# x turned by a transposing DMA, the last keys' values paired otherwise, and the adapter's output product at another place

## The chip, the cores and the metric

The kernel runs on one core of a Trainium2 chip. The metric is the device time of one execution in microseconds (us); every time below is in us unless ns stands beside it. The engines are PE (matmul; PEld is its weight load), DVE (vector), ACT (scalar, exponentials), POOL (general) and SP, which in this kernel only issues DMAs.

## The reference

Attention with a relative position bias, for 8 batches, 8 heads, 576 positions and head width 64; then a mixture of low-rank adapters on the 4608 rows of 512 that it gives.

```python
scores = q @ k.T / sqrt(64) + bias_table[bucket(|i - j|)]
attn = softmax(scores)                          # over the keys
x = (attn @ v) laid out as (8 * 576, 512)
logits = x @ w_gate                             # 8 experts
w = softmax of the two largest logits           # the two experts kept
out = x + sum over the two of w * ((x @ A[e]) @ B[e])   # A: 512 x 16, B: 16 x 512
```

## The kernel before

The work is cut into 32 **units**, u = 4 b + hp, of one batch b and one pair of heads hp. Of the 576 positions of a batch 512 are the main part, in four tiles of 128, and 64 are the tail. The scores are computed with the keys on the partitions: `keys(u, c)` gives a block of 128 keys against 512 queries of both heads (tile `sc`, L353 and L358; the bias enters as a product with a table), `keys_exp` its exponential on ACT (`pk`, L364). `edges(u)` gives the scores of tail keys and tail queries (L395, L400) and their exponential `pt` (L402), which `edge_bias` corrects on POOL (L408) and DVE (L410).

Score tiles take turns in three PSUM buffers of two banks, six tiles a unit: two `keys`, a third, the turning of the next unit's q and k (`tp`), the fourth `keys`, and the next unit's `edges`. All else that PE writes goes to the pool `mp` (tag `mm`) of two buffers with one bank each: values (`pv`), the adapter's output product (`dl`), the corner scores (`cps`), turned x (`xT_ps`), logits of a whole group (`zl`).

The values, attn @ v with a column of ones for the sums, are computed a unit late, in two groups. `values_a` (tiles 0, 1, 2) and `values_b` (tile 3 and the tail) each fill one `pv` tile; `pv_main` (L418) adds a block of main keys, `pv_last` (L428) the tail keys, `pv_tail` (L442) is for the tail's queries. Tiles 0 and 2 can share a weight load in `pv_last`, as can 1 and 3, since tail keys of two batches lie on the two halves of the partitions. `normalise_a` and `normalise_b` divide by the sums on DVE and write x: `xs[b]` for the main part, `xe[b // 2]` for the tails of two batches.

The adapter works on **groups**: two tiles of x (g0: tiles 0 and 1; g1: 2 and 3), or the tail rows of two batches. For each group x is turned (`turn_x`, L334, and `copy_x`, L338), multiplied with the first adapter matrices and the gate (`moe_z`, L499, in the free columns of a `pv` tile from `values_b`, or `moe_zpair`, L507), gated on DVE, POOL and ACT, and turned again (`moe_t`, L559, `moe_tc`, L562); `moe_d` (L566, L569) makes the output product `dl`, adds x and, when a group is complete, issues the store on SP's queue.

The order of everything is written out by hand in the loop over u; the engines take their instructions in that order. Dictionaries hold which group's step comes in which unit. With u the first unit of batch b, `moe(b - 1, u)` puts the steps of batch b - 1 there: g0 is turned in unit u + 1, g1 in u + 2, a tail group in u + 3; `moe_z` for the four tiles comes in u + 2 to u + 5, `moe_d` (dictionary `second`) in u + 5 to u + 8. For batch 6 the turns come in u and u + 1, each followed by `moe_zpair` at the end of the same unit. Batch 7 is done after the loop, in code that the change does not touch.

In a unit, the order on PE is: two `keys`; `moe_d`; `values_b` of the unit before with `moe_z`; transposes of x; the third `keys`; the turning of q and k (and `cps` in a batch's first unit); the fourth `keys`; `values_a` of the unit before with `moe_t`; `edges` of the next unit. In unit 28 `values_a` comes directly behind `values_b`.

SP issues in program order the loads of q and k four units ahead and of v three units ahead, the tails a batch ahead, and the stores. A DMA whose data is not ready holds up all behind it.

## Time and profile before

| | |
|---|---|
| median of three runs | 205.93 us (204.39 to 206.39) |
| profiled execution, its own time | 205.11 us |
| span of its profile | 203.3 us |
| granted PE clock | 0.998 of full speed |
| PE, PEld busy | 173.8, 127.5 us (86%, 63%) |
| ACT, DVE, POOL busy | 166.1, 138.3, 130.9 us (82%, 68%, 64%) |
| moved by DMA | 39.87 MB, mean 196 GB/s |

The span runs from the first to the last instruction of the profiled execution; the 1.8 us between it and the execution's own time lie around it. A busy share is a mean over stages. Idle time of an engine stands in the profile with the releaser, the instruction that ended it; the chain is followed back from the last instruction through these releasers.

### The profile page before, as it was taken

What the parts mean: (1) busy time and instruction counts of PE and PEld (TensorE: products, weight loads), DVE (VectorE), ACT (ScalarE), POOL (GpSimd) and SP (SyncE); (2) the same over time, 40 slices, a digit from 0 to 9 for tenths busy, and PEclk for the clock granted to TensorE, in tenths of its full rate; (3) what the DMA queues carried; (4) which work ended last, traced back from release to release, by engine and by line L of the source; (5) the groups of instructions that cost most, each with busy time, mean ns of one, the idle gap of its engine ahead of it and who ended that gap; (6) DMA issues with size and microseconds to landing.
All of it is one profiled execution on the core that took longest, in us unless ns stands there. A gap on an engine that the chain in (4) does not pass through costs nothing.

```text
span 203.3 us, 11419 instructions
## 1 busy us (share of the span) xinstructions
PE 173.8 (86%) x4898; PEld 127.5 (63%) x4898; DVE 138.3 (68%) x411; ACT 166.1 (82%) x205; POOL 130.9 (64%) x321
## 2 busy tenths in 40 slices
PE   0377889899999899989988999999988997999870
PEld 0255666677666677766676677767776685666640
DVE  4314655467667876887877777789877786888750
ACT  3269999998998889989879889889988878788470
POOL 4298546678578647986694947985776577761110
PEclk9999999999999999999999999999999999999999
DMA  5868889679778886855279999862498940042165
GB/s 134 214 192 240 235 243 240 177 212 272 213 208 254 252 218 203 242 173 158 58 196 299 280 242 295 251 203 72 108 280 262 291 167 24 3 157 107 55 241 173
DMA packets 62714, 39.87 MB, mean 196 GB/s; under 512 B 17848, under 2 KB 59336, under 8 KB 62664
## 3 DMA queue, kind: packets, MB, share of 16 engines
q1 hardware_dynamic: 61864, 38.58, 64.7%
q8 instruction: 38, 0.62, 1.3%
q10 hardware_dynamic: 800, 0.56, 1.1%
q14 instruction: 12, 0.10, 0.2%
HBM read 29.67 MB, written 9.46 MB: 192 GB/s over the span
## 4 chain that ended last, share of the span: by engine, by line
PE 51%; ACT 18%; DVE 15%; issue 5%; DMA 5%; POOL 2%; ACTq 0%; POOLq 0%; DVEq 0%
PE pv L418 14%; PE sc L353 10%; ACT pk L364 10%; ACT pt L402 6%; PE sc L358 5%; DVE ot L569 5%; PE xT_ps L334 4%; PE pv L428 3%; PE sc L395 3%; PE tp L302 3%; DVE pt L410 2%; PE sc L400 2%; PE dl L566 2%; PE pv L442 2%; DMA Wt<-g_d 1%
## 5 line engine op out<-in xcount | busy, mean ns | idle before, releaser
L364 ACT ACTIVATE pk<-sc 128x1024 bf16<-128x1024 f32 x128 | 124.1, 1028 | 14.6 <-PE sc L358 13.4
L353 PE MATMUL sc<-qkT 64*64 64x512 bf16 x512 | 52.8, 396 | 3.4 <-ACT pk L364 2.7
L418 PEld LDWEIGHTS <-pk 128*128 128x128 bf16 x1024 | 38.7, 98 | 16.4 <-issue 7.8
L358 PE MATMUL sc<-Wt,anti 64*64 64x384 bf16 (+1 forms) x512 | 44.1, 300 | 1.8 <-DMA Wt<-g_d 1.8
L418 PE MATMUL pv<-v,pk 128*128 128x65 bf16 x992 | 42.7, 194 | 0.9 <-DVE z L522 0.4
L402 ACT ACTIVATE pt<-sc 128x1024 bf16<-128x1024 f32 x32 | 32.8, 1024 | 10.3 <-PE sc L400 5.2
L306 DVE COPY qkT<-tp 128x1024 bf16<-128x1024 bf16 x32 | 22.0, 686 | 6.9 <-PE tp L302 6.2
L410 DVE TENSOR_TENSOR pt<-pt,ET 64x256 bf16<-64x256 bf16 x32 | 15.3, 477 | 15.2 <-ACT pt L402 11.9
L353 PEld LDWEIGHTS <-qkT 64*64 64x64 bf16 x512 | 17.1, 106 | 12.7 <-issue 5.7
L137 POOL CAST v<-vs 128x512 bf16<-128x512 f32 x32 | 20.4, 637 | 6.6 <-DMA vs<-in_v_dram 6.5
L141 POOL CAST kn<-ks 128x512 bf16<-128x512 f32 x31 | 19.4, 626 | 1.1 <-PE sc L358 0.9
L358 PEld LDWEIGHTS <-anti 64*64 64x64 bf16 x512 | 17.9, 108 | 2.9 <-issue 2.9
L569 DVE TENSOR_TENSOR ot<-dl,xn 128x512 f32<-128x512 f32 x25 | 17.3, 691 | 1.3 <-PE dl L566 0.3
L477 DVE TENSOR_TENSOR xn<-pv,rc 128x384 bf16<-128x384 f32 x31 | 17.3, 557 | 1.1
L141 POOL CAST qn<-qs 128x512 bf16<-128x512 f32 x27 | 16.6, 613 | 1.6 <-PE sc L358 0.9
L428 PE MATMUL pv<-vb,pt 128*128 128x65 bf16 (+1 forms) x186 | 17.5, 203 | 0.0
L302 PEld LDWEIGHTS <-qn 64*64 64x64 bf16 x512 | 10.8, 111 | 10.4 <-ACT qn L141 5.3
L532 POOL TENSOR_TENSOR a<-z,top 128x16 f32<-128x16 f32 (+1 forms) x17 | 3.8, 223 | 19.2 <-DVE top L527 19.1
L302 PE MATMUL tp<-ident,qn 64*64 64x64 bf16 x512 | 11.1, 196 | 5.7 <-ACT qn L141 5.3
L562 DVE COPY zT<-pv 128x128 bf16<-128x128 bf16 x31 | 6.7, 221 | 12.0 <-PE pv L559 12.0
L408 POOL TENSOR_TENSOR pt<-pt,ELC 128x128 bf16<-128x128 bf16 x32 | 13.8, 431 | 1.5 <-ACT pt L402 1.4
L442 PE MATMUL pv<-v,pt 128*128 128x65 bf16 x248 | 13.0, 193 | 0.0
(147 smaller groups left out, 337.8 us busy)
## 6 DMA issues: line engine op xcount, KB each, us to landing
qs<-in_q_dram SPq DMA_DIRECT2D x32, 256.0 KB, 3.9
vs<-in_v_dram SPq DMA_DIRECT2D x64, 128.0 KB, 4.0
ks<-in_k_dram SPq DMA_DIRECT2D x62, 128.0 KB, 3.8
out_dram<-ot SPq DMA_DIRECT2D x11, 512.0 KB, 4.2
vt<-in_v_dram SPq DMA_DIRECT2D x8, 128.0 KB, 4.1
out_dram<-fot SPq DMA_DIRECT2D x4, 256.0 KB, 2.4
qkt<-in_q_dram SPq DMA_DIRECT2D x7, 128.0 KB, 4.7
qkt<-in_k_dram SPq DMA_DIRECT2D x7, 128.0 KB, 3.9
```

Of the source, the lines that this page charges most:

```text
L137: eng.tensor_copy(t[:, :, :, :D].rearrange("p c h d -> p h c d"), s)
L141: copy(t.rearrange("p c h d -> p h c d"), s)
L302: nc.tensor.transpose(self.ps[h * 64:h * 64 + 64, f, x * 64:x * 64 + 64], src[rows, h * 64:h * 64 + 64], ident[rows, rows])
L306: nc.vector.tensor_copy(_ap(dst, 0, [[64, 2], [128, n], [1, 64]]), self.ps[:, :, x * 64:(x + n) * 64].rearrange("p f (x t) -> p f x t", t=64))
L353: nc.tensor.matmul(sc[prt, h, :], lhsT=kT[rows, c * 128 + f * 64:c * 128 + f * 64 + 64], rhs=qT[rows, :], start=True, stop=False, skip_gro ...
L358: nc.tensor.matmul(_ap(sc[prt, h, :], p0, [[128, 4], [1, n]]), lhsT=turned(h), rhs=_ap(Wt[rows, hp, :], (1 - e) * GY + y0, [[GY, 4], [1, n]]),
L364: nc.scalar.activation(probs[u][0][c], scs.pop(c), ACT.Exp, scale=scale)
L402: nc.scalar.activation(probs[u][1][:, 64:], sc.rearrange("p h x -> p (h x)"), ACT.Exp, scale=scale)
L410: eng.tensor_tensor(te, te, ET[64:, :, hp, :], op=ALU.mult)
L418: nc.tensor.matmul(pv[:, o + h * W1:o + (h + 1) * W1], lhsT=pk[c][:, h, t * 128:(t + 1) * 128], rhs=vm[:, c, h, :], start=(first and h == ...
L428: nc.tensor.matmul(_ap(pv, o + h * W1, [[260, n], [1, W1]]), lhsT=pt[:, x0:x0 + 128], rhs=tvs[b % 2][:, t // 2:t // 2 + n, 2 * hp + h, :], ...
L569: nc.vector.tensor_tensor(gr.ot[:, t, :], dl, gr.x[t], op=ALU.add)
```

## The change

Three edits come together.

1. `turn_x` issues one transposing DMA on SP's queue, from x in SBUF to `xT` in SBUF. The transposes on PE, their PSUM tile `xT_ps` and `copy_x` on DVE go. The place in the program order stays.
2. `values_a` does tiles 0 and 2 and the tail's queries, `values_b` tiles 1 and 3, so that each has one `pv_last` with shared weight loads. The normalising is divided in the same way.
3. The dictionary `second`, that is `moe_d`, runs after the fourth `keys`, ahead of `values_a`, instead of ahead of `values_b`.

```diff
     def turn_x(gr):
         n = len(gr.x)
-        gr.xT_ps = mp.tile([128, 2, 4, 128], BF16, name="xT_ps", tag="mm")
-        for i, x in enumerate(gr.x):
-            for c in range(4):
-                nc.tensor.transpose(gr.xT_ps[:, i, c, :], x[:, c * 128:(c + 1) * 128], ident)
-
-    def copy_x(gr):
-        gr.xT = xtp.tile([128, len(gr.x), 4, 128], BF16, name="xT", tag="xT")
-        nc.vector.tensor_copy(gr.xT, gr.xT_ps[:, :len(gr.x)])
+        gr.xT = xtp.tile([128, n, 4, 128], BF16, name="xT", tag="xT")
+        nc.sync.dma_start_transpose(out=gr.xT.rearrange("p n c t -> p (n c) t"), in_=gr.flat)
...
     def pv_last(u, pv, o, t, n=1):
...
-            nc.tensor.matmul(_ap(pv, o + h * W1, [[260, n], [1, W1]]), lhsT=pt[:, x0:x0 + 128],
+            nc.tensor.matmul(_ap(pv, o + h * W1, [[130, n], [1, W1]]), lhsT=pt[:, x0:x0 + 128],
...
     def values_a(u):
         pva[u] = mp.tile([128, 512], FP32, name="pv", tag="mm")
-        for t in range(3):
+        for t in (0, 2):
             for c in range(4):
-                pv_main(u, pva[u], t * 130, t, c, t == 0 and c == 0)
+                pv_main(u, pva[u], t * W1, t, c, t == 0 and c == 0)
         pv_last(u, pva[u], 0, 0, 2)
-        pv_last(u, pva[u], 130, 1)
+        for c in range(5):
+            pv_tail(u, pva[u], c, 260)
         return pva[u]
 
     def values_b(u):
         pvb[u] = mp.tile([128, 512], FP32, name="pv", tag="mm")
-        for c in range(4):
-            pv_main(u, pvb[u], 0, 3, c, c == 0)
-        pv_last(u, pvb[u], 0, 3)
-        for c in range(5):
-            pv_tail(u, pvb[u], c)
+        for t in (1, 3):
+            for c in range(4):
+                pv_main(u, pvb[u], (t - 1) * W1, t, c, t == 1 and c == 0)
+        pv_last(u, pvb[u], 0, 1, 2)
         return pvb[u]
...
+    def norm_pair(u, pv, rc, t, i):
+        b, hp = units[u]
+        nc.vector.tensor_tensor(_ap(xs[b], t * Dm + hp * 128, [[2 * Dm, 2], [D, 2], [1, D]]),
+                                _ap(pv, 0, [[2 * W1, 2], [W1, 2], [1, D]]),
+                                _ap(rc, i, [[2, 2], [1, 2], [0, D]]), op=ALU.mult)
+
     def normalise_a(u):
...
-        nc.vector.tensor_tensor(_ap(xs[b], hp * 128, [[Dm, 3], [D, 2], [1, D]]),
-                                _ap(pv, 0, [[2 * W1, 3], [W1, 2], [1, D]]),
-                                _ap(rc, 0, [[2, 3], [1, 2], [0, D]]), op=ALU.mult)
+        norm_pair(u, pv, rc, 0, 0)
+        rows = slice(64 * (b % 2), 64 * (b % 2) + 64)
+        nc.vector.tensor_tensor(xe[b // 2][rows, hp * 128:hp * 128 + 128].rearrange("p (h d) -> p h d", h=2),
+                                _ap(pv[rows], 260, [[W1, 2], [1, D]]), _ap(rc[rows], 4, [[1, 2], [0, D]]),
+                                op=ALU.mult)
 
     def normalise_b(u):
...
-        nc.vector.tensor_tensor(_ap(xs[b], 3 * Dm + hp * 128, [[D, 2], [1, D]]),
...
+        norm_pair(u, pv, rc, 1, 6)
...
             gr.x = [xs[b][:, c, :] for c in (2 * i, 2 * i + 1)]
+            gr.flat = xs[b][:, 2 * i:2 * i + 2, :].rearrange("p c d -> p (c d)")
...
             gr.x = [xe[b // 2]]
+            gr.flat = xe[b // 2]
...
         if u == 6:
             weights_turn(1)
-        run(second.pop(u - 1, []))
...
             if early:
                 normalise_a(u - 1)
-            else:
-                for gr in xg:
-                    copy_x(gr)
...
             run(after.pop(u, []))
+            run(second.pop(u - 1, []))
             if not early:
                 pa = values_a(u - 1)
             else:
                 for gr in xg:
                     turn_x(gr)
-                    copy_x(gr)
```

More of the change, by code (lines that the diff above doesn't have):

```diff
@@ L427, in pv_last, with pv_tail @@
             x0 = 64 + h * SM + 256 + t % 2 * 128
-            nc.tensor.matmul(_ap(pv, o + h * W1, [[260, n], [1, W1]]), lhsT=pt[:, x0:x0 + 128],
+            nc.tensor.matmul(_ap(pv, o + h * W1, [[130, n], [1, W1]]), lhsT=pt[:, x0:x0 + 128],
                              rhs=tvs[b % 2][:, t // 2:t // 2 + n, 2 * hp + h, :], start=False, stop=False,
                              skip_group_check=True)
-    def pv_tail(u, pv, c, o=130, first=False):
+    def pv_tail(u, pv, c, o, first=False):
         b, hp = units[u]
@@ L484, in normalise_b @@
         nc.vector.reciprocal(rc[:, 6:], _ap(pv, D, [[W1, 4]]))
-        nc.vector.tensor_tensor(_ap(xs[b], 3 * Dm + hp * 128, [[D, 2], [1, D]]),
-                                _ap(pv, 0, [[W1, 2], [1, D]]),
-                                _ap(rc, 6, [[1, 2], [0, D]]), op=ALU.mult)
-        rows = slice(64 * (b % 2), 64 * (b % 2) + 64)
-        nc.vector.tensor_tensor(xe[b // 2][rows, hp * 128:hp * 128 + 128].rearrange("p (h d) -> p h d", h=2),
-                                _ap(pv[rows], 130, [[W1, 2], [1, D]]), _ap(rc[rows], 8, [[1, 2], [0, D]]),
-                                op=ALU.mult)
+        norm_pair(u, pv, rc, 1, 6)
     class Group:
```

## The prediction

> **What bounds the kernel now.** I read the page first (busy shares, the chain by line), then the stretches between two units, then the chain in order of time, last SP's queue.

> ```profile
> span 203.3 us, 11419 instructions
> PE 51%; ACT 18%; DVE 15%; issue 5%; DMA 5%; POOL 2%; ACTq 0%; POOLq 0%; DVEq 0%
> ```

> No engine bounds it alone: the chain changes between PE, ACT and DVE. So the unit of account is one unit of the loop (one batch and head pair). Each ends with the 24 matmuls of `values_a` (L418), which stand in the chain and serve as a clock; unit 17's start at 107.14, unit 20's at 123.53. Stretches between such marks (columns: PE, PEld, DVE, ACT, POOL busy, clock, DMA share, GB/s):

> ```profile
> 52.72:57.72 5.00, 4.66 (x148) 3.39 (x146) 3.48 (x12) 4.69 (x7) 2.87 (x9) 1.00 0.68 179
> 107.14:112.99 5.85, 5.26 (x150) 3.82 (x148) 4.39 (x13) 5.08 (x7) 3.50 (x10) 1.00 1.00 300
> 112.99:118.49 5.50, 5.05 (x161) 3.79 (x160) 3.91 (x13) 4.95 (x6) 3.82 (x8) 1.00 0.93 286
> 118.49:123.53 5.04, 5.03 (x149) 3.55 (x148) 4.05 (x13) 4.71 (x7) 2.84 (x9) 1.00 0.86 219
> 123.53:129.15 5.62, 5.62 (x154) 4.31 (x152) 4.14 (x14) 5.08 (x8) 5.23 (x14) 1.00 0.97 297
> ```

> A unit that turns x (5.85, 5.50, 5.62) is 0.5 to 0.8 longer than one that does not (5.00, 5.04). The chain says why. First a short unit, then a turning one:

> ```profile
> 52.20 0.41 PE sc L353 x4
> 52.61 0.11 PE sc L358 x2
> 52.72 0.93 PE pv L418 x24
> 53.65 0.18 PE pv L428 x4
> 53.83 0.23 PE sc L395 x4
> 54.06 0.12 PE sc L400 x16
> ...
> 55.21 1.95 ACT pk L364 x2
> ...
> 57.20 0.41 PE sc L353 x4
> ```
> ```profile
> 109.83 0.68 DVE pt L410
> ...
> 110.54 0.70 DVE ot L569
> ...
> 111.28 0.61 PE xT_ps L334 x8
> 111.89 0.34 PE sc L353 x4
> ```

> In the short unit two legs follow each other. On PE: the last `keys` (0.52), `values_a` (1.11), `edges` (0.35). On ACT: the exponential of the edges and the first two of the keys, after which a score tile is free for the last `keys` again. ACT itself stands idle ahead of the edges, so the PE leg counts in full:

> ```profile
> 54.29 1.02 ACT L402 ACTIVATE pt<-sc 128x1024 bf16<-128x1024 f32 x1 [0.31 <-POOL sm L536]
> ```

> The releaser named there is POOL; I read it as the edges' matmuls, which end at 54.18. In the turning unit another way is longer: edges' exponential, DVE's product on it, then `ot` behind it, which frees the misc PSUM tile that the transposes need.

> ```profile
> PE xT_ps L334 <- DVE ot L569: 5.7, 11, 0.7
> L338 DVE COPY xT<-xT_ps 128x1024 bf16<-128x1024 bf16 (+1 forms) x17 | 10.7, 630 | 1.0 <-PE xT_ps L334 1.0
> ```

> **The change, part by part.**

> *Transposes and copies removed.* Each full group takes 0.61 off PE and one copy off DVE (17 copies, 10.7 us). DVE's time is worth nothing by itself. What it is worth on the path is the difference between a turning unit and what bounds the unit next. Were that 5.04, units 9 to 27 (57.72 to 162.14, 104.4 us for 19) would lose 8.6.

> *The product `dl` moved.* Now it stands between the first two `keys` and `values_b`, where PE waits for DVE's product on the edges anyway: unit 20 has it there and takes 5.04. After the change it stands between the last `keys` and `values_a`, on the PE leg of the loop, in every unit from 9 to 31. Its cost there is its step in the chain, and the short transpose of `zt` adds 0.06:

> ```profile
> 121.00 0.32 PE dl L566
> 119.58 0.06 PE pv L559
> ```

> So a unit becomes 5.00 + 0.34 + 0.06 = 5.40, whether it turns x or not. In the first unit of a batch a second price comes: the misc pool has two buffers, and there `pv`, `cps` and now `dl` come ahead of `values_a`. One of the last two must take the buffer of `cps`, which is free only when ACT has read it:

> ```profile
> 122.94 1.03 ACT L364 ACTIVATE pk<-sc 128x1024 bf16<-128x1024 f32 x1
> 123.51 0.95 PE L418 MATMUL pv<-v,pk 128*128 128x65 bf16 x24
> 123.84 0.41 ACT L376 ACTIVATE pcx<-cps 128x256 bf16<-128x256 f32 x1
> ```

> ACT leaves it at 124.25. PE would be through `dl` at 123.51 + 0.34 = 123.85, so it waits 0.4 to 0.5; such a unit (12, 16, 20, 24) becomes 5.86. Sum over units 9 to 27: 15 x 5.40 + 4 x 5.86 = 104.4, what they take now. The saving of the turning units is spent on the others. Below, `dl` could be worth nothing (5.04 stays); above, 0.39, its whole duration. I take the chain's step.

> *Values paired.* `values_a` has 24 + 4 = 28 matmuls now and 16 + 2 + 10 = 28 after; `values_b` goes from 20 to 18, ahead of a wait. DVE's pieces are regrouped (three ops and four, as now). Zero, bounds -0.05 and +0.05 a unit.

> *The DMA.* No transposing DMA is in this trace. Nearest rows, from issue to landing:

> ```profile
> qs<-in_q_dram SPq DMA_DIRECT2D x32, 256.0 KB, 3.9
> vt<-in_v_dram SPq DMA_DIRECT2D x8, 128.0 KB, 4.1
> out_dram<-fot SPq DMA_DIRECT2D x4, 256.0 KB, 2.4
> ```

> The load of q has the size of a turn of two tiles; `vt` moves runs of 256 bytes, as a turn does (128 values of 2 bytes). The lower bound is 2.4, a quiet queue; the upper 8.2, two transfers like `vt` one after the other. I take 3.9 on a busy queue and 2.4 on an idle one. In most batches this is hidden: x is ready just after a batch's first unit, its consumer `moe_z` comes over a unit later. It is not hidden where SP comes late, since the DMA is issued behind the loads of its unit:

> ```profile
> 98.88 1.19 SPq L578 DMA_DIRECT2D out_dram<-ot  x2
> ...
> 105.70 0.42 SPq L589 DMA_DIRECT2D out_dram<-ot  x1
> 106.21 0.39 SPq L113 DMA_DIRECT2D qs<-in_q_dram  x1
> ...
> 108.32 1.06 SPq L110 DMA_DIRECT2D vs<-in_v_dram  x2
> 110.29 0.40 PE L499 MATMUL pv<-AW,xT 128*128 128x136 bf16 x4
> ```

> SP waits for the tail's `ot` until 98.88, then works through unit 16's eight loads and a store until 106.1 and unit 17's loads until 109.4; only there would the turn of batch 3 be issued. That is 11.6 after the edges' exponential of unit 16 (97.77). Two units of 5.86 and 5.40, and 1.85 to `moe_z` in unit 18, give 13.1. Room 1.5, need 3.9: PE stands 2.4 if SP is as slow as now, about 1.2 if longer units take the back-pressure off SP (its loads took 3.2 where 2.5 is their sum undisturbed). I take 1.8, and 2.2 for batch 5, where SP's same stretch is 0.5 longer. Everything behind `moe_z` on PE (two `keys`, the turning of q and k) waits too, then ACT, so it counts in full. Batch 5's tail is turned and used in the same unit 27: 0.8, the rest lies beside ACT.

> Batch 6 is turned in unit 28 and used at its end:

> ```profile
> 165.89 0.36 SPq L589 DMA_DIRECT2D out_dram<-ot  x1
> 168.99 0.61 PE L334 MATMUL xT_ps<-ident,xn 128*128 128x128 bf16 x8 [0.70 <-ACT pcx L376]
> 169.63 0.69 DVE L338 COPY xT<-xT_ps 128x1024 bf16<-128x1024 bf16 x1 [0.97 <-PE xT_ps L334]
> 170.38 0.65 PE L507 MATMUL zl<-AW,xT 128*128 128x136 bf16 x8 [0.37 <-DVE xT L338]
> ```

> The store at 165.89 belongs to a product that moves behind the last `keys`, to some 169.4, and the turn is queued behind it: issue at 169.8, landing at 172.2 against 170.38, +1.8. Unit 29 drops 0.6 of transposes from a PE that is busy throughout, unit 6 the 0.5 that it has in the chain:

> ```profile
> 46.19 0.45 PE xT_ps L334 x8
> ```

> Sum: 0 - 0.5 - 0.6 + 1.8 + 2.2 + 0.8 + 1.8 = +5.5. The profiled execution took 205.11 (span 203.3 and 1.8 around it), 0.8 below the median 205.93. 205.1 + 5.5 = 210.6; I say 210.5, and leave the 0.8 to the range.

> The row of q gives 3.9 for a plain 256 KB. [...]

> **Rivals.** *In time, and the product hidden* (faster): landing near 2.4, and `dl` finds idle time on PE, as it does in unit 20 now. Then units take 5.04, minus 8.6, minus 0.5 (unit 6), minus 0.6 (unit 29), plus 1.8 in unit 28: 197. For it: PE is 4.66 busy in 5.00. Against: ACT's idle time ahead of the edges shows that PE's leg has no slack. It holds if units fall below 5.2.

> *In time, product on the path*: units at 5.40, landing 2.4, so the late places cost 0.3, 0.7, 0 and 1.8, less 1.1: 206.8. For it: the queue can be that quick after the loads thin out. Against: DMA share 1.00 at 107 to 113, just there.

> *Slow turns*: landing 6 to 8.2. Units 18, 26 and 28 wait 2 to 6 longer each; units 14 and 22, where the turn is issued some 3 after the unit before begins and 7.3 ahead of `moe_z`, wait 1.7 to 3.9; in units 6 and 10, issued at 0.9, at most 1.8: 221 to 236. For it: 17 more transfers of many short runs. Against: `vt` lands in 4.1 with runs as short.

> *No effect at all*: the turn is not done by DMA, or PE still carries the transposes: 2%.

> **How the numbers follow.** Forecast 40%, faster rival 22%, product on the path but in time 18%, slow turns 18%, no effect 2%. About 1% is what a measurement of this kernel can tell from no change (203.9 to 208.0). Faster: 0.22. Same: 0.20. Slower: 0.58. The likeliest case alone has 207 to 214 (landing 3 to 5); the range that reaches to the others is 197 to 220 and leaves out the slow turns.

> **What would show it.** Right: the short chain in every unit with `dl` between `sc` L353 and `pv` L418; units of 5.3 to 5.5, batches' first units near 5.9 with a wait for `pcx`; PE at `moe_z` in units 18 and 26, and at `zl` in unit 28, waiting for the DMA that writes `xT`; landing 3 to 5. Wrong: units near 5.05, no wait for `xT`, or such waits in every batch.

## The result, and the profile after

| | before | after |
|---|---|---|
| median | 206.16 us (204.39 to 206.82, 4 runs) | 235.53 us (232.03 to 236.23, 4 runs) |
| ratio, 95% interval | 1 | 1.133 (1.124 to 1.142) |
| profiled execution, its span | 205.11, 203.3 us | 235.47, 233.6 us |
| granted PE clock | 0.998 | 0.937 |

The changed kernel takes 29 us more by the medians of all runs, and 27 by the ratio, which leaves out the executions that fell into a slower state. 210.5 had been forecast, with 197 to 220 as the range. The page of the changed kernel gives the first hint: the busy times of PE and ACT have hardly moved (173.8 to 178.0 and 166.1 to 165.9), but the transfer that writes `xT` stands in the chain that ended last, and the clock has dips.

```profile
span 233.6 us, 11065 instructions
PEclk9999999988999999799995999999985995899998
PE 41%; DMA 19%; ACT 18%; DVE 7%; issue 6%; POOL 3%; SPq 2%; ACTq 0%; POOLq 0%
```

DMA had 5% of the chain before and has 19% now. The waits by PE's lines (total, times, longest) say where it stands, and the list of DMA issues how long the transfer is (KB are not given for it; the last number is the median time from issue to landing):

```profile
PE pv L497 <- DMA xT<-xn: 18.3, 5, 5.6
PE zl L505 <- DMA xT<-xn: 4.6, 1, 4.6
PE zl L505 <- DMA xT<-xe: 1.0, 1, 1.0
```
```profile
xT<-xn SPq DMA_TRANSPOSE x14, 4.6
xT<-xe SPq DMA_TRANSPOSE x3, 3.6
```

Seven of the 17 turns are late for their reader (`moe_z`, L497, and `moe_zpair`, L505), by 23.9 in all. The five at L497 stand in units 6, 14, 18, 22 and 26. Below, the length of a unit u is the time from the start of the exponential of its edges to that of the next unit's, read from ACT's timeline of each kernel.

| unit | before | after | e1 | e2 | e4 | e5 | e8 |
|---|---|---|---|---|---|---|---|
| 6 | 5.86 | 11.03 | 5.85 | 12.02 | 6.20 | 8.56 | 7.92 |
| 14 | 5.78 | 8.58 | 5.72 | 7.46 | 5.52 | 5.21 | 6.36 |
| 18 | 5.80 | 12.43 | 5.58 | 12.03 | 5.22 | 10.30 | 5.22 |
| 22 | 5.58 | 6.20 | 5.72 | 8.36 | 5.21 | 5.22 | 7.02 |
| 26 | 5.80 | 12.08 | 5.22 | 11.46 | 5.79 | 10.36 | 5.22 |
| 28 | 6.32 | 6.84 | 7.18 | 8.09 | 5.79 | 5.79 | 13.54 |
| 29 | 6.44 | 12.03 | 6.73 | 7.14 | 6.18 | 11.96 | 12.70 |
| 9 to 27 | 104.4 | 120.9 | 104.2 | 115.5 | 105.1 | 113.2 | 106.3 |

(e1: x turned on PE again; e2: the transposing DMA alone; e4: nothing waits for `xT`; e5: turn issued ahead of the loads; e8: stores later as well. All are told below.) After against before, the span grows by 30.3: unit 6 +5.2, 14 +2.8, 18 +6.6, 22 +0.6, 26 +6.3, units 28 to 30 +6.7, the other 15 units from 9 to 27 +0.2 together, what follows unit 30 +1.9.

Unit 18 shows what such a wait does. First PE, with the idle time and its releaser in brackets; then stretches of two microseconds (behind the length of the stretch stand the busy times of PE, PEld, DVE, ACT and POOL; the last three numbers are granted clock, DMA share, GB/s):

```profile
117.67 0.28 PE L423 MATMUL pv<-vb,pt 128*128 128x130 bf16 x2
123.52 0.64 PE L497 MATMUL pv<-AW,xT 128*128 128x136 bf16 x4 [5.58 <-DMA xT<-xn]
126.05 0.61 PE L564 MATMUL dl<-Bc,zT 128*128 128x512 bf16 x1
```
```profile
118.00:120.00 2.00, 0.00 (x0) 0.00 (x0) 0.00 (x0) 1.57 (x3) 0.22 (x1) 1.00 0.90 252
122.00:124.00 2.00, 0.48 (x4) 0.36 (x4) 0.00 (x0) 0.00 (x0) 0.54 (x1) 0.52 1.09 275
124.00:126.00 2.00, 2.00 (x50) 1.08 (x48) 1.29 (x4) 0.85 (x1) 0.61 (x2) 0.50 1.11 250
128.00:130.00 2.00, 2.00 (x54) 1.41 (x52) 0.94 (x4) 0.96 (x2) 0.62 (x1) 0.77 0.88 272
```

PE stands 5.58, and then works at half the clock until some time after 128: `dl` takes 0.61 where it takes 0.39 elsewhere. Unit 18 is 12.43, where a unit of its kind without a wait is 5.26 (unit 17); 7.2 lost for a wait of 5.6. On SP's queue the turn of that batch (its issue at 118.40) stands behind this:

```profile
101.55 0.93 SPq L110 DMA_DIRECT2D vs<-in_v_dram  x2
106.98 2.04 SPq L576 DMA_DIRECT2D out_dram<-ot  x2
...
114.94 0.35 SPq L588 DMA_DIRECT2D out_dram<-ot  x1
...
117.36 0.93 SPq L110 DMA_DIRECT2D vs<-in_v_dram  x2
118.40 2.37 SPq L333 DMA_TRANSPOSE xT<-xn  x1
```

SP issues nothing between 102.5 and 107.0 (it stands at the store of a tail, L576), has three tail loads, ten unit loads and another store to issue, and reaches the turn at 118.40, when PE has already been standing for its result since 117.94.

A unit that waits for no x looks as forecast. The chain in unit 10, the waits for `cps`, and the stretches of units 10 and 12 (the second is a batch's first unit; in it, at 84.58, PE waits 0.40 for ACT to have read `cps`):

```profile
70.77 1.94 ACT pk L359 x2
...
72.75 0.41 PE sc L348 x4
73.16 0.11 PE sc L353 x2
73.27 0.37 PE dl L564
73.64 0.51 PE pv L413 x16
```
```profile
PE pv L413 <- ACT pcx L371: 1.6, 4, 0.4
```
```profile
69.85:75.06 5.21, 4.74 (x144) 3.32 (x139) 3.44 (x12) 4.78 (x6) 3.13 (x8) 1.00 0.94 146
80.38:86.16 5.78, 5.04 (x146) 3.51 (x139) 3.45 (x12) 5.06 (x7) 3.60 (x9) 1.00 0.75 167
```

### The profile page after: what moved, and what is told of

The parts are those of the page before. It is cut to its first block, busy times and chain, and to the rows that moved or that the text cites. A ratio compares the mean times of both kernels' runs of the same rounds, so it can differ in the third digit from the quotient of the medians.

```text
span 233.6 us, 11065 instructions
## 1 busy us (share of the span) xinstructions
PE 178.0 (76%) x4711; PEld 125.3 (54%) x4712; DVE 126.4 (54%) x394; ACT 165.9 (71%) x205; POOL 131.2 (56%) x321
## 4 chain that ended last, share of the span: by engine, by line
PE 41%; DMA 19%; ACT 18%; DVE 7%; issue 6%; POOL 3%; SPq 2%; ACTq 0%; POOLq 0%
ACT pk L359 14%; DMA xT<-xn 11%; PE sc L348 10%; PE pv L413 10%; PE sc L353 5%; PE pv L437 4%; PE dl L564 3%; PE sc L390 2%; SPq L110 2%; DMA vs<-in_v_dram 2%; PE pv L423 2%; DMA xT<-xe 2%; PE pv L497 2%; DVE qkT L306 1%; PE tp L302 1%
## 5 line engine op out<-in xcount | busy, mean ns | idle before, releaser
L348 PE MATMUL sc<-qkT 64*64 64x512 bf16 x512 | 55.4, 415 | 8.2 <-ACT pk L359 7.6
L353 PE MATMUL sc<-Wt,anti 64*64 64x256 bf16 (+1 forms) x512 | 46.3, 315 | 2.2 <-DMA Wt<-g_d 2.2
L413 PE MATMUL pv<-v,pk 128*128 128x65 bf16 x992 | 44.1, 197 | 3.2 <-ACT pcx L371 1.6
L348 PEld LDWEIGHTS <-qkT 64*64 64x64 bf16 x512 | 18.9, 110 | 19.1 <-issue 12.2
L471 DVE TENSOR_TENSOR xn<-pv,rc 128x256 bf16<-128x256 f32 x62 | 26.3, 424 | 2.1
L497 PE MATMUL pv<-AW,xT 128*128 128x136 bf16 x96 | 10.4, 235 | 18.3 <-DMA xT<-xn 18.3
L488 DVE RECIPROCAL rc<-pv 128x4 f32<-128x4 f32 x31 | 5.7, 184 | 30.5 <-PE pv L497 22.2
L353 PEld LDWEIGHTS <-anti 64*64 64x64 bf16 x512 | 18.9, 112 | 3.0 <-issue 2.9
L405 DVE TENSOR_TENSOR pt<-pt,ET 64x256 bf16<-64x256 bf16 x32 | 12.0, 374 | 13.3 <-ACT pt L397 9.7
L423 PE MATMUL pv<-vb,pt 128*128 128x130 bf16 x124 | 17.8, 226 | 0.0
L497 PEld LDWEIGHTS <-xT 128*128 128x128 bf16 x96 | 6.8, 102 | 19.2 <-DMA xT<-xn 19.2
## 6 DMA issues: line engine op xcount, KB each, us to landing
qs<-in_q_dram SPq DMA_DIRECT2D x32, 256.0 KB, 4.1
vs<-in_v_dram SPq DMA_DIRECT2D x64, 128.0 KB, 4.1
ks<-in_k_dram SPq DMA_DIRECT2D x62, 128.0 KB, 3.8
vt<-in_v_dram SPq DMA_DIRECT2D x8, 128.0 KB, 3.9
out_dram<-fot SPq DMA_DIRECT2D x4, 256.0 KB, 4.7
qkt<-in_q_dram SPq DMA_DIRECT2D x7, 128.0 KB, 3.3
qkt<-in_k_dram SPq DMA_DIRECT2D x7, 128.0 KB, 3.8
```

The lines of the kernel that those rows point to most:

```text
L348: nc.tensor.matmul(sc[prt, h, :], lhsT=kT[rows, c * 128 + f * 64:c * 128 + f * 64 + 64], rhs=qT[rows, :], start=True, stop=False, skip_gro ...
L353: nc.tensor.matmul(_ap(sc[prt, h, :], p0, [[128, 4], [1, n]]), lhsT=turned(h), rhs=_ap(Wt[rows, hp, :], (1 - e) * GY + y0, [[GY, 4], [1, n]]),
L413: nc.tensor.matmul(pv[:, o + h * W1:o + (h + 1) * W1], lhsT=pk[c][:, h, t * 128:(t + 1) * 128], rhs=vm[:, c, h, :], start=(first and h == ...
L423: nc.tensor.matmul(_ap(pv, o + h * W1, [[130, n], [1, W1]]), lhsT=pt[:, x0:x0 + 128], rhs=tvs[b % 2][:, t // 2:t // 2 + n, 2 * hp + h, :], ...
L471: nc.vector.tensor_tensor(_ap(xs[b], t * Dm + hp * 128, [[2 * Dm, 2], [D, 2], [1, D]]), _ap(pv, 0, [[2 * W1, 2], [W1, 2], [1, D]]), _ap(rc ...
L497: nc.tensor.matmul(zl, lhsT=gr.xT[:, t, c, :], rhs=AW[:, c, :], start=False, stop=(c == 3), skip_group_check=True)
```

## The experiments

**The three edits apart.** e1 takes the first edit back and leaves the other two; e2 has the first alone; e3 the second alone.

e1_pe_turn, against the changed kernel:

```diff
     def turn_x(gr):
-        nc.sync.dma_start_transpose(out=gr.xT..., in_=gr.flat)
+        (transposes on PE into xT_ps, copy_x on DVE, as before)
```

> The changed kernel with x turned on PE and copied by DVE again; pairing and the product's new place stay. Theory (the turn by DMA comes late and PE waits for it): no wait of 4 to 6 is left, time 205 to 212, PE's clock 1.0 throughout; a turning unit takes 5.5 to 6.0, the others 5.2 to 5.3, first units of a batch 5.8. Rival (the product's place or the pairing costs the 30): 225 or more.

Measured: 209.74 us (209.19 to 210.31), ratio 1.016 (1.010 to 1.023). Units 9 to 27 take 104.2 against 104.4 before; units 28 to 30 are 1.7 longer, and unit 0 is 1.2 longer in this profile.

e2_dma_only, against the kernel before: only `turn_x` by DMA, `copy_x` gone.

> The kernel before with the turn by DMA alone; pairing and the product's place as before. Theory: the waits for xT in units 6, 14, 18, 22, 26 and 28 stay, 225 to 235; units without a wait take 5.0 to 5.1, since no product stands on PE's leg. Rival (product's place or pairing costs the 30): 200 to 208.

Measured: 225.20 us (221.76 to 227.71). Of the units from 9 to 27 those without a late turn take 5.00 to 5.06 (but 5.31 in unit 16 and 5.39 in unit 24), and seven readers wait, five of them at `moe_z`:

```profile
PE pv L493 <- DMA xT<-xn: 20.3, 5, 6.0
```

e3_pair_only, against the kernel before: `values_a` with tiles 0 and 2 and the tail, `values_b` with 1 and 3.

> The kernel before with the pairing of the values alone. As forecast: two matmuls fewer in values_b, ahead of a wait, and the same number in values_a: 205 to 207, no difference that can be told. Rival (pairing shortens or lengthens every unit by 0.1 or more): 203 or 209.

Measured: 206.93 us (205.83 to 210.12), ratio 1.007 (1.003 to 1.010). In its profile units 9 to 27 are the same to 0.02; the 1.3 that its unit 0 takes more stands in the start-up, as in e1.

What follows: the loss is the DMA's; the two others cost one or two per cent together. In e2 the 15 units from 9 to 27 that are not 14, 18, 22 or 26 save 5.3, where the bound of 5.04 a unit gives 5.9; so the transposes were worth about what had been worked out, and the waits cost several times as much.

**The transfer, or the wait for it.** e4 lets every turn be issued as in the changed kernel, but nobody reads its result.

```diff
-            nc.tensor.matmul(zl, lhsT=gr.xT[:, t, c, :], rhs=AW[:, c, :], start=False,
+            nc.tensor.matmul(zl, lhsT=sel[:, c * 128:(c + 1) * 128], rhs=AW[:, c, :], start=False,
...
-                nc.tensor.matmul(zl[:, t, :], lhsT=gr.xT[:, t, c, :], rhs=AW[:, c, :],
+                nc.tensor.matmul(zl[:, t, :], lhsT=sel[:, c * 128:(c + 1) * 128], rhs=AW[:, c, :],
```

> The changed kernel, but the products that make the logits read a constant tile in place of turned x, so that nothing in the loop waits for the turn; the DMAs are still issued and moved (the logits, and with them the adapter's part of the output, are left out of the computation). Theory: 203 to 208, clock 1.0 throughout. Rival (the 17 transfers themselves, by taking SP's and the DMA engines' time, make loads late and slow the loop): 215 or more, with waits of POOL's casts for loads.

Measured: 207.06 us (206.84 to 209.65), ratio 1.008 (1.003 to 1.013), clock 0.995. With all 17 transfers on the queues and no reader the kernel is 28 us faster: the waits and the clock behind them are the loss, not the traffic.

**Why the turn is late: its place behind the unit's loads?** e5 issues the turn ahead of the loads of its unit.

```diff
+        xg = [g for g, in tx.pop(u, [])]
+        if not (b == B - 1 and hp == 0):
+            for gr in xg:
+                turn_x(gr)
         if hp == 0 and 0 < b < B - 1:
             load_tail(b + 1)
```

> The changed kernel with the turn issued on SP ahead of its unit's five loads instead of behind them (unit 28's stays where it is). Theory: it is issued some 3 earlier, so the waits in units 6, 14 and 22 go and those in 18 and 26 fall from 5.6 to about 2.3, too short for the clock to fall; unit 28's wait stays: 212 to 218. Rival (the transfer itself is slow whenever it is issued, or crowds out the loads): 228 or more.

Measured: 225.77 us (223.93 to 228.32), ratio 1.091 (1.082 to 1.100).

```profile
PE pv L497 <- DMA xT<-xn: 9.7, 3, 4.3
PE zl L505 <- DMA xT<-xn: 4.6, 1, 4.6
```

Units 14 and 22 are in time, as expected; units 6, 18 and 26 still wait. The forecast of 212 to 218 missed: the five loads are a part of the lateness, and the larger part lies farther up the queue. That about 2.3 would be too short for the clock to fall was the author's guess: 2.55 idle in unit 14 of the changed kernel brought 0.50, and so did the 3.45 in unit 18 here.

**The clock.** e6 puts 80 matmuls of a constant ahead of `moe_z` in units 6, 18 and 26 of the changed kernel, so that PE's idle time is shorter.

```diff
+            if u in (6, 18, 26):
+                for _ in range(80):
+                    nc.tensor.matmul(pv[:, 400:464], lhsT=ident, rhs=ident[:, :64], start=False, ...)
```

> The changed kernel with 80 further matmuls on PE (some 3.1, into columns that nobody reads) right ahead of the wait for turned x in units 6, 18 and 26. If the clock falls because PE stands idle for 4 to 6, the idle time is now 1 to 2.5, the clock stays at 1.0 there, and each of these units ends about 2 earlier though PE does more: 228 to 231, granted clock above 0.97. Rival (the clock falls for another reason, or its fall costs nothing): 235 or more, clock near 0.94.

Measured: 234.42 us (232.08 to 235.47). Unit 18 in its timeline and stretches:

```profile
117.46 2.50 PE L747 MATMUL pv<-ident 128*128 128x64 bf16 x80
123.47 0.41 PE L497 MATMUL pv<-AW,xT 128*128 128x136 bf16 x4 [3.52 <-DMA xT<-xn]
```
```profile
122.00:124.00 2.00, 0.53 (x8) 0.38 (x12) 0.08 (x1) 0.00 (x0) 0.21 (x1) 1.00 1.04 285
124.00:126.00 2.00, 2.00 (x73) 1.49 (x66) 1.97 (x6) 1.51 (x2) 1.17 (x2) 1.00 1.23 286
```

The x lands at the same time (PE goes on at 123.47 instead of 123.52), the clock stays at 1.00, and the unit takes 10.47 instead of 12.43. So about 2 of unit 18's loss is the clock, 2.1 in unit 26. Unit 6 gained only 0.3: the clock stayed at 1.00 there too, but x landed 1.15 later (PE goes on at 51.21 instead of 50.06), with the turn issued at the same time. The total hardly moved, since units 22, 28 and 29 were 1.5, 3.2 and 1.4 longer in that profile; the expectation for the total was wrong. Why engines that run earlier find x later there was not followed up: it fits SP as the pacemaker, but is not shown.

**Another queue.** e7 issues the turns on ACT's queue, at the same place in the program order.

```diff
-        nc.sync.dma_start_transpose(out=gr.xT..., in_=gr.flat)
+        nc.scalar.dma_start_transpose(out=gr.xT..., in_=gr.flat)
```

> The changed kernel with one word different: the 17 turns are issued on ACT's queue instead of SP's, at the same place in the program order (on ACT that is between the second and the third exponential of the unit's keys; x is ready there). Theory A, SP's place in its queue is what makes x late, not the transfer: the loads and stores ahead of it no longer count, so x lands 4 to 5 after the exponentials, in time for units 6, 14, 18, 22 and 26; no PE wait for xT over 0.5 there, the granted clock stays at 1.00 there; batch 6 (zl in the unit of the turn) still waits, 1 to 4. ACT pays 17 issues: 0.1 each if they only start the transfer, 1.25 each if they occupy ACT as they occupy SP; most of that on the path, since ACT's leg bounds the short unit. Time 208 to 218. Theory B, the transfer itself is slow or crowded out (landing 5 to 8 from whichever queue): the waits in 18 and 26 shrink but stay over 1, and the time is above 220.

Measured: 235.69 us (231.69 to 236.84), no gain. Theory A holds for the waits in units 18 and 26, which are gone; units 6, 14 and 22 still wait 0.9, 1.7 and 1.2, where none over 0.5 was expected (`moe_z` waits 3.8 in all instead of 18.3). It fails in the total, since ACT now stands instead. Unit 18, ACT:

```profile
122.22 0.23 ACT L543 ACTIVATE th<-sm 128x16 f32<-128x16 f32 x1
125.19 1.25 ACTq L333 DMA_TRANSPOSE xT<-xn  x1
126.54 1.94 ACT L359 ACTIVATE pk<-sc 128x1024 bf16<-128x1024 f32 x2 [4.09 <-DMA vs<-in_v_dram]
```

The turn reads nothing of `vs`, yet what ended ACT's 4.09 of idle time is, by the trace, the landing of a load of v that SP had issued. SP's waits in this run name landings too, 3.8 at its stores (L588) for `vs` and 2.9 at its loads (L110) for `xT`. So a load on SP's queue held up ACT; by what way an issue on one queue comes to wait for a transfer of the other is not shown. One issue takes 1.25 on ACT's queue as well (median of the 14 turns of two tiles; 1.31 on SP's in the changed kernel).

**What makes SP late.** Two readings stood against each other by now: a store whose rows are not ready, which holds up what is queued behind it (in the changed kernel SP stood at the tail's store from 102.5 to 107.0), or a queue that is full, whatever stands in front, which was a guess of the author's that no run shows. e8 is e5 with the stores moved down SP's order.

```diff
         elif not gr.left:
-            gr.store(gr.ot)
+            if now[0] < 26:
+                pend.append((now[0] + (2 if len(gr.x) == 1 else 1), gr))
+            else:
+                gr.store(gr.ot)
...
         if u + 3 < NU:
             load(u + 3, "v")
+        flush(u)          # stores that are due, behind the loads of unit u
```

> The changed kernel with the turn issued ahead of the unit's loads, and besides the stores put later in SP's order: a store of main rows behind the loads of the next unit, a tail's two stores behind those of the unit after that (from unit 26 on as it was). Theory A, SP is late in units 14, 18, 22 and 26 because a store whose rows are not ready yet (SP stands 4 to 5 ahead of the tail's, up to 3 ahead of each other one) holds up the loads and the turn behind it: with the stores out of the way the turns of units 9 to 26 are issued when x is ready, no wait for xT over 0.5 in units 9 to 27, granted clock 1.00 there, units 18 and 26 at 5.2 to 5.3 instead of 10.3; units 6, 28 and 29 still wait as with the turn first alone. Time 212 to 218 (225.8 less twice 5, with 2 to either side). [...]

Measured: 219.22 us (216.47 to 224.63), ratio 1.057 (1.051 to 1.064), 1.2 above the range of theory A. The profiled execution took 224.63, 5 over the median; what is read from it here are units 9 to 27, where its clock was 1.00. SP and PE in batch 3:

```profile
107.20 1.28 SPq L333 DMA_TRANSPOSE xT<-xn  x1
...
112.39 1.18 SPq L586 DMA_DIRECT2D out_dram<-ot  x2
```
```profile
113.16 0.40 PE L497 MATMUL pv<-AW,xT 128*128 128x136 bf16 x4
```

The turn is issued 0.5 after the edges' exponential of unit 17 (106.72), ahead of the tail's store, and PE finds x there; units 18 and 26 take 5.22. For these two units that decides for the stores. Waits of 1.1 and 1.8 remain in units 14 and 22, where the expectation said none over 0.5, and 2.3 in unit 6; what is left there is not explained. The longest in this profile are 6.0 for the tail group that is turned in unit 27 and 4.6 for batch 6, where turn and reader stand in one unit.

**Versions from it.** All are the kernel before with some groups turned by DMA, issued ahead of the unit's loads; neither the pairing nor the product's new place is in them.

| | turned by DMA | stores | median | ratio to before |
|---|---|---|---|---|
| c1 | g1 of batches 0 to 6, all three tails | as before | 204.53 | 0.988 (0.980 to 0.996) |
| c2 | and g0 of batches 1, 2, 4 | as before | 206.45 | 0.998 (0.993 to 1.002) |
| c3 | as c1, without batch 5's tail | as before | 203.13 | 0.989 (0.985 to 0.993) |
| c4 | as c3, and g0 of batch 1 | as before | 203.76 | 0.984 (0.980 to 0.989) |
| c5 | as c3, and g0 of batches 1 to 5 | later, as in e8 | 205.13 | 0.996 (0.992 to 1.000) |

```diff
-                for gr in xg:
+                for gr in pg:              # the groups that PE turns
                     turn_x(gr)
...
+        gr.pe = i == 0                     # c1; c3: or (i == 2 and b == 5)
```

> The kernel before, with the turn by DMA only for the groups that have over a unit to spare (g1 and the tails), issued ahead of its unit's loads; g0 is turned on PE as before; product and values as before. Theory: no wait for xT; units 6, 10, 11, 14, 18, 19, 22, 26 and 27 fall to 5.05 to 5.3, which gives 5 to 6: 199 to 202. Rival (the transfers on SP make something else late): 206 or more.

> As the one before, but g0 too is turned by DMA in batches 1, 2 and 4, where the run with the turn issued first had no wait; on PE stay g0 of batches 0, 3, 5 and 6. Theory: units 9, 13 and 21 fall to 5.05 as well: 1.4 less than the one before, 198 to 201. Rival (with units at 5.05 SP is late again): waits for xT in units 10, 14 or 22, 204 or more.

> The kernel before, with only the g1 groups of batches 0 to 6 and two tail groups turned by DMA (issued ahead of the unit's loads); all g0 groups and batch 5's tail group are turned on PE as before. The kernel that turned batch 5's tail by DMA too had 204.5 and 10.1 in unit 28, where the kernel before has 6.3. Theory A: those 3.8 are the wait for that tail and the slow clock behind it, so they go: 200.5 to 203, unit 28 at 6.2 to 6.5, units 10, 14, 19, 26, 27 at 5.0 to 5.1. Theory B: unit 28 was long for another reason (batch 6's turn in units 28 and 29, which still go by DMA for g1): unit 28 or 29 stays over 8 and the time at 204 to 206.

> As the kernel with g1 and two tails by DMA, and batch 1's g0 by DMA as well (in the kernel that had g0 of three batches by DMA this one did not make PE wait, and its unit took 5.06 instead of 5.44). Theory A, the gain is per turn that lands in time: 0.3 to 0.4 less than its neighbour without it, 200 to 203. Theory B, a turn more on SP's queue makes a later one late: a wait for xT of over 1 in unit 10 or 11, and 0.5 to 3 more than its neighbour.

> The kernel before with the groups of batches 1 to 5 (g0 and g1) and g1 of batches 0 and 6 turned by DMA ahead of the unit's loads, batch 5's tail, and g0 of batches 0 and 6, on PE; stores later in SP's order as in the run beside it. Theory A (stores made SP late): every turning unit from 9 to 26 takes 5.0 to 5.1, no wait for xT: 198 to 202. Theory B (queue full): units 14, 18, 22 or 26 wait again, 203 to 212.

A group g1 is turned half a batch after x is ready, so its turn has slack. In c1 units 10, 14, 19, 26 and 27 take 5.0 to 5.1, but unit 28 takes 10.1 in the profiles of c1 and c2, where PE waits 2.4 and 2.3 for batch 5's tail, turned in unit 27, and the clock falls behind it (0.71 from 166 to 168 in c1, 1.00 again from 168 on). Not every execution need show it: two of c1's four took 202.43 and 203.57, within c3's range. c3 turns that tail on PE: unit 28 is 7.0, and the stretches of units 10 and 19 (before: 5.80 and 5.55) are

```profile
66.13:71.16 5.03, 4.51 (x145) 3.43 (x142) 3.66 (x12) 4.78 (x6) 3.38 (x8) 1.00 1.08 192
...
114.43:119.48 5.05, 4.86 (x161) 3.69 (x158) 3.89 (x13) 4.69 (x5) 3.60 (x10) 1.00 1.02 284
```

c2 brings the waits back in units 14 and 22 (6.4 and 9.1). c5 loses there too: four readers wait, 6.8 in all, and the longest wait, 3.5 in unit 22, makes that unit 4.1 longer than before. SP stands at no store there: from 120.99 on it issues one store and eight loads, one right after the other, and then at 127.88 the turn of unit 21, which had begun at 121.86. So stores are not the whole of SP's lateness, and what the rest is, a full queue as the rival had it or something else, is not shown.

```profile
131.93 0.41 PE L503 MATMUL pv<-AW,xT 128*128 128x136 bf16 x4 [3.47 <-DMA xT<-xn]
```

c3 and c4 beat both kernels, by 1.1 and 1.6 per cent; the intervals of the two overlap. That c4 is faster than c3, by 0.3 to 0.4 as expected, is not shown: its six runs fall into two clusters, 201.20 to 202.67 and 204.85 to 206.29, the ratio rests on the first, and the median of all six is above c3's. The medians of both lie just above the ranges expected, 203.1 where 200.5 to 203 had been said and 203.8 where 200 to 203; in c3 unit 28 kept 0.7 of what should have gone. c1, c2 and c5 missed by more: 199 to 202, 198 to 201 and 198 to 202 had been the theory's ranges, and c2 and c5 came out as their rivals said. Nor is the gain of c3 the sum of its turned units: units 10, 14, 18, 19, 22 and 26 save 3.7 together, units 9 to 27 only 2.1, since others, such as 12 and 24, grew by 0.5 each; why is open.

## Why the prediction was wrong

**Right: the cycle of a unit.** It was to become 5.40, and 5.86 in a batch's first unit, by `dl` on PE's leg and the wait for `cps`. Measured: 5.21 to 5.32, and 5.78; units 15 and 23, at 5.61 with x turned by DMA or on PE, are not explained. The sum over units 9 to 27 was to stay as it is; e4, where nothing waits for x, has 105.1 for 104.4, and in the changed kernel the 15 units that are not late for x differ by 0.2. The rule for turning units also held: in e2 they go to 5.05, as the bound had it. The pairing was put at zero: in e3 units 9 to 27 bear that out, though the whole kernel took 0.7 per cent more.

**Wrong: the step "in most batches this is hidden".** It said that SP comes late only in batches 3 and 5. It came late in 0, 2 and 4 too. For units 14 and 22 the working put the issue 7.3 ahead of the reader; in unit 14 it was 2.2 ahead (issue 90.53, PE ready at 92.76):

```profile
90.53 1.49 SPq L333 DMA_TRANSPOSE xT<-xn  x1
...
95.31 0.63 PE L497 MATMUL pv<-AW,xT 128*128 128x136 bf16 x4 [2.55 <-DMA xT<-xn]
```

Unit 6 was entered as a gain of 0.5. SP is a unit behind from the start-up, and the turn of batch 0, whose reader was free at 46.0, is issued at that very moment, 2.6 into unit 6 instead of in unit 5:

```profile
46.11 1.36 SPq L333 DMA_TRANSPOSE xT<-xn  x1
...
50.06 0.41 PE L497 MATMUL pv<-AW,xT 128*128 128x136 bf16 x4 [4.03 <-DMA xT<-xn]
```

The prediction read SP's timeline at two places and took the rest for granted. These three units are 8.6 of the 30.

**Mis-sized: units 18 and 26**, +1.8 and +2.2, measured +6.6 and +6.3. The steps of unit 18, counted from the edges' exponential of unit 16 (105.57): issue at 12.8, 11.6 taken (the tail's store came 0.3 later, the rows behind it 0.9); reader at 12.4, 13.1 taken (the units were shorter, and `moe_z` stands 1.3 into its unit, not 1.85; in the kernel before it stood 1.5 in, 110.29 less the unit's start at 108.76); landing 5.1, 3.9 taken. In the chain, the two batches:

```profile
118.40 5.08 DMA xT<-xn
...
170.31 4.37 DMA xT<-xn
```

1.2, 0.7 and 1.2 on top of the 2.4 that it allowed make the 5.6 of the trace. Each slip is small; the room was smaller. The clock adds the rest, about 2 in each (e6): no step of the sum had it.

**Mis-sized: batch 6.** +1.8 became a wait of 4.6, shown here with the issue:

```profile
192.63 0.35 SPq L588 DMA_DIRECT2D out_dram<-ot  x1
193.08 2.98 SPq L333 DMA_TRANSPOSE xT<-xn  x2
...
196.86 1.09 PE L505 MATMUL zl<-AW,xT 128*128 128x136 bf16 x8 [4.57 <-DMA xT<-xn]
```

The landing was 3.7, not the 2.4 of an idle queue. And the working compared it with the old start of `zl`, which had transposes and a copy ahead of it; with these gone PE is there 0.8 ahead of the issue, not 0.6 behind it. That the store ahead of the turn would hold it up was right. Batch 5's tail, 0.8, came out at 1.0.

**The rivals.** "Slow turns" had 221 to 236 and named units 6, 14 and 22. The number and the places fit, the mechanism does not: landings were 3.3 to 5.2, not 6 to 8, and what was slow was SP. e8 tells the two apart: its landings were longer (median 5.4), and units 18 and 26 had no wait. The faster rival needed units below 5.2; they were at 5.2 to 5.3.

**The landing.** The row of q stood for the turn, with 3.9. In the changed kernel a turn of two tiles lands in 4.6 in the median, a q load of the same size in 4.1 (3.9 before): near, by landing. The row says nothing of the issue, where the two differ, 1.31 against 0.53 in the median.

## What to carry to other kernels

The turn that was moved to SP's queue took that queue's place in time: SP issued nothing from 102.5 to 107.0, where the tail's store waited for its rows, and reached unit 18's turn at 118.40, when PE had been standing for it since 117.94. So list what stands ahead of each issue, and first of all the stores. Compare issue, landing and first need for every instance, not for the two worst, and count a room of 1.5 as none: unit 18's ended as a wait of 5.6. Where room is real (g1 here) the same edit gains; where turn and reader stand a unit apart behind a busy queue, it cost up to 6.6 us a time to save 0.6.

## What the runs showed of the hardware

```profile
91.37:94.78 3.41, 1.39 (x34) 0.91 (x26) 1.02 (x3) 2.96 (x4) 3.13 (x9) 1.00 1.13 200
94.78:98.20 3.42, 2.89 (x54) 1.66 (x54) 1.60 (x6) 1.10 (x2) 3.22 (x7) 0.50 1.16 293
```
```profile
142.21:145.62 3.41, 2.20 (x66) 1.54 (x62) 1.48 (x6) 2.97 (x4) 3.33 (x10) 1.00 1.35 128
145.62:149.04 3.42, 1.92 (x54) 1.08 (x54) 1.62 (x7) 1.44 (x4) 3.02 (x8) 1.00 1.15 295
149.04:152.45 3.41, 3.29 (x91) 2.70 (x95) 2.03 (x8) 2.54 (x3) 2.28 (x4) 1.00 1.28 211
```

- A transposing DMA of 256 KB in SBUF lands in 3.3 to 5.2 among the loads of the changed kernel (the tails' turns of 128 KB counted in; up to 6.6 in e7), but its issue occupies the queue for 1.24 at least and 1.31 in the median, where the load of q, of 256 KB too, has 0.37 and 0.53:

```profile
L333 SPq DMA_TRANSPOSE xT<-xn x14: 1242/1311/2527, 46.1 to 194.6; - x14
...
DMA to landing us min/median/max: 3.3/3.9/5.2
```

- Left open: why unit 0 takes 10.2 to 10.7 in the profiles of e1, e3, e7, c1, c2 and c4, and 9.2 to 9.7 in the others. PE waits there for a table's DMA; no edit stands at that place.
